# Convolution groups moved from the matrix engine to GpSimd and VectorE in a windowed attention with a gated unit

## The chip, the cores and the metric

One Trainium2 chip, one of its cores. A core has a matrix engine (TensorE, PE in the profile), VectorE (DVE), ScalarE (ACT), GpSimd (POOL) and SyncE (SP), which here only issues transfers. The metric is the device time of one execution in microseconds; lower is better. Times before are the median of three runs.

## The reference

Attention over 8 sequences, 8 heads, 576 positions, 64 dimensions, then a gated unit over the 512 joined channels:

```python
scores = (q @ k.T) / sqrt(64)
rel = pos[:, None] - pos[None, :]
mask_plain = (rel >= 0) & (rel < 32)                       # heads 0 to 3
mask_dil = (rel >= 0) & (rel < 128) & (rel % 4 == 0)       # heads 4 to 7
attn = softmax(where(mask, scores, -1e9))
x = (attn @ v).transpose(0, 2, 1, 3).reshape(B, S, 512)
gate_pre = sum_k conv_w[k] * x shifted by (4 - k) positions   # 5 taps, causal, one weight a channel
out = (sigmoid(gate_pre) * (x @ w_val)) @ w_out
```

Inputs and outputs are float32.

## The kernel before

The kernel is a list of 733 small tasks. Functions (`plain`, `dilated`, `attend`, `gated`, `outputs`, `weights`) add tasks to a plan in a fixed numbering, each with the engines that may run it, the tasks it depends on and the buffers it uses. `ORDER` then says, task by task, in which order and on which engine the instructions are written, and `HOMES` gives each buffer its place in a ring (`COUNTS` has the sizes: three double PSUM banks `ps2`, two single ones `ps1`, three `wt`, three `gate`, two `vp`, and so on). Each engine runs its tasks in that order; waits between engines follow from the buffers. A digit behind a P is a number of idle matmuls written ahead of the task.

Work is staged by pairs of sequences (g = 0 to 3). For each sequence the four plain and the four dilated heads are done two heads at a time:

- loads of q, k and v on SyncE's queue (lines 270 to 302; a large load waits for the fifth large load before it, `DEPTH`), transposes of q and k on TensorE into PSUM (L401 plain, L464 dilated), copies from PSUM into `qT` and `kT` on ScalarE (L312) or VectorE (L314). Dilated v is cast whole by GpSimd (`U`, into `vn`); plain v of the first four sequences is shifted and cast (`HA` to `HD`, into `vw`) by GpSimd or ScalarE (L316, L312).
- `attend`: scores (L333), exp on ScalarE (L340), the mask product on VectorE (L347, both inputs in SBUF), the product with v (L356), and the normalisation on VectorE (L365 reciprocal, L366 product). Transposes (L428, L488) and copies (`F` tasks) bring the result to `xT`, channels by positions.
- `gated`: for each pair the 1152 positions are cut in three blocks of 384 (four of 288 for the last pair), and each block in two channel pairs cp of two 128-channel chunks n. That makes 26 groups. In a group, `C` computes the five-tap convolution of both chunks as 20 matmuls of 64 x 64 diagonal weights (L530), `G` takes the tanh on ScalarE out of PSUM (L540), `V` is the projection in 8 matmuls (L548), and `Y` multiplies on VectorE (L558). Since channel halves lie crossed in the second chunk, its convolution also swaps partitions 0-63 and 64-127.
- `outputs`: 36 row blocks of four matmuls (L577), eviction by ScalarE (L584) or VectorE (L586), store on SyncE's queue (L590).

Weights are loaded through the `wt` buffers and cast by GpSimd (`Wv`, `Wo`).

Of the kernel before, what the change touches and what calls it, by code (L numbers as in the profile page):

```python
# [7 lines left out]
FP32 = mybir.dt.float32  # L8
BF16 = mybir.dt.bfloat16
# [7 lines left out]
0G 15S 16S 1S 13S 33P6 14S 34A 48S 17S 47S 49S 2P 31P1 32A 3V 18G 38P2 57P 51G 21P 59V 22V 53G 58V 52G 39A 40V  # L17
19P 35P 20A 26P2 36A 23P 80S 27A 37V 24A 28V 25V 41P2 54P 56A 4S 55A 42V 29P 30V 70P 81S 6G 45P3 5G 43P 50A
60P 73P 7S 46V 71A 44A 74A 8G 112S 61A 96P 84P 63P 64A 149P 72V 97A 75V 76P 98P 85V 65V 62V 82S 66P 77V 86P
67V 150A 99A 100P 78P 87A 101A 83G 103P 88P 89A 79V 68P 69V 104A 113S 105V 119P 114S 120A 91P 92A 145P 151P  # L20
93V 102V 90V 121A 94P 169S 146A 152V 106P 95V 147P 122P 107V 108P 170S 110P 123V 124A 138P 109A 201S 139A 148V
135P 185P 136A 125P 128P 129A 126A 111V 165P 166A 140V 130V 137V 116G 127V 186V 234S 202S 157P 158A 187P 115G
118G 117G 141P 171S 175P 176A 188V 192P 193A 131P 142V 132V 173P 172G 174A 189P 190A 208P 209V 210A 143P 133P
177P 178A 180P 203S 134V 211P 235S 250P 144V 159P 181A 213A 212A 227P 228A 153P 154A 11S 238P 205G 251V 194V
179V 191V 160V 182V 239A 206A 195P 229V 196V 207A 167P 168V 204G 12G 183P 184V 155P 252P 224P 225A 214P 240P
215A 9S 253V 156V 199P 254P 241V 255A 226V 217P 218A 161P 230P 197P 162A 200A 324S 267S 236S 216V 219V 245P
256V 220P 198A 246A 231V 10G 625P 628P 221V 323S 266S 325S 237G 626A 257P 242P 243A 276P 629A 222P 326G 223A
258A 278A 277V 163P 341P 232P 303P 247V 244V 259V 233V 342V 304A 299P 300A 164V 339P 260P 248P 329P 305P 330A
340V 268S 261V 631P 630S 355S 384S 533S 627S 346P 356S 249V 343P 264P 306V 265V 273P 632A 347A 344A 348V 274V
275A 272A 345V 262P 301P 302V 279P 280A 292P 634P 635V 263A 349P 350V 327P 293A 328A 289P 281V 282P 283A 290A  # L30
# [33 lines left out]
 'gate': 3,  # L64
 'osb': 5,
 'xT': 3,
 'yT': 3,
 'vw': 2,
 'wt': 3}
DEPTH = 5  # L70
NAT = 4


def hi_bf16(ap: bass.AP) -> bass.AP:
    b = ap.bitcast(BF16)
    idx = tuple([slice(None)] * (len(b.shape) - 1) + [slice(1, None, 2)])
# [632 lines left out]
```

## Time and profile before

| | us |
|---|---|
| median of three runs (lowest to highest) | 174.27 (173.8 to 174.28) |
| profiled execution | 173.37 |
| its span, first to last instruction | 171.7 |
| TensorE, matmuls busy | 153.0 |
| VectorE busy | 121.7 |
| ScalarE busy | 108.4 |
| GpSimd busy | 44.2 |

The mean granted clock of TensorE is 0.998. Transfers move 43.63 MB at a mean of 254 GB/s. Reading the rows: a group has its line, engine, operation, output and input tile, their shapes and the count; then total busy time and mean ns of one; then the engine's idle time just before, with what ended it. A row of the table by stage has the stage, its length, and for each engine the busy time and the count of instructions.

### The profile page before, as it was taken

The numbers are of one execution on the slowest core, as the hardware profiler recorded it, in microseconds if no ns is written. First come the engines' busy times: TensorE is split into PE (matmuls) and PEld (weight loads), VectorE is DVE, ScalarE is ACT, GpSimd is POOL, SyncE is SP. The second block draws the span as 40 slices with busy tenths as digits, with TensorE's granted clock in tenths as the row PEclk, the third lists the DMA queues.
The fourth block names the chain that finished last, engine by engine and source line by source line (L and its number), as shares of the span: only waits on it lengthen the run. The fifth ranks groups of instructions, "written<-read, shape, count | busy, mean of one in ns | idle before, by whom it ended". The sixth has DMA issues, their size and how long they took to land.

```text
span 171.7 us, 5752 instructions
## 1 busy us (share of the span) xinstructions
PE 153.0 (89%) x2441; PEld 102.2 (60%) x2460; DVE 121.7 (71%) x243; ACT 108.4 (63%) x182; POOL 44.2 (26%) x82
## 2 busy tenths in 40 slices
PE   6697967888989979899999799989999999999990
PEld 1355654677557546567766567576656577666640
DVE  6549778989899579779788658899368776664220
ACT  2147976198868744798847693888946675242542
POOL 7023998560659427403000000210110000000000
PEclk9999999999999999999999999999999999999999
DMA  4999999999799999999994948969979060333445
GB/s 137 325 355 290 375 370 210 311 374 319 200 383 364 362 269 281 373 353 222 282 328 139 267 115 286 373 165 390 270 202 303 2 244 4 116 119 138 186 165 199
DMA packets 49123, 43.63 MB, mean 254 GB/s; under 512 B 22981, under 2 KB 39365, under 8 KB 49098
## 3 DMA queue, kind: packets, MB, share of 16 engines
q1 hardware_dynamic: 49098, 43.27, 82.2%
q8 instruction: 19, 0.31, 0.7%
q14 instruction: 6, 0.05, 0.1%
HBM read 33.83 MB, written 9.44 MB: 252 GB/s over the span
## 4 chain that ended last, share of the span: by engine, by line
PE 58%; DMA 12%; DVE 11%; ACT 6%; SPq 5%; issue 3%; POOL 3%; ACTq 0%; DVEq 0%; POOLq 0%
PE pu L577 17%; PE pd L548 14%; PE pd L530 9%; DMA qk<-in_k_dram 5%; PE pd L356 5%; DVE et L347 4%; DMA wt<-in_moe_w_out_dram 4%; SPq L281 4%; PE pd L333 4%; DMA qk<-in_q_dram 3%; PE pu L464 3%; POOL w_out L316 3%; PE pd L401 2%; PE pu L488 2%; ACT et L340 2%
## 5 line engine op out<-in xcount | busy, mean ns | idle before, releaser
L340 ACT ACTIVATE et<-pd 128x576 bf16<-128x576 f32 x64 | 39.3, 657 | 10.4 <-PE pd L333 9.3
L347 DVE TENSOR_TENSOR et<-et,mask 128x576 bf16<-128x576 bf16 x64 | 33.9, 557 | 4.7 <-ACT et L340 4.5
L548 PE MATMUL pd<-xT,w_val 128*128 128x384 bf16 (+1 forms) x208 | 34.9, 313 | 0.7 <-DVE xn L366 0.4
L577 PE MATMUL pu<-w_out,yT 128*128 128x512 bf16 x127 | 33.4, 379 | 1.4 <-issue 0.6
L558 DVE SCALAR_TENSOR_TENSOR yT<-gate,pd 128x768 bf16<-128x768 bf16 (+1 forms) x26 | 23.0, 886 | 12.5 <-PE pd L548 8.5
L366 DVE TENSOR_TENSOR xn<-pd,rec 96x768 bf16<-96x768 f32 x32 | 30.5, 954 | 1.1
L316 POOL CAST vn<-vd 128x1536 bf16<-128x1536 f32 x8 | 12.3, 1540 | 70.3 <-DMA vd<-in_v_dram 70.3
L540 ACT ACTIVATE gate<-pd 128x768 bf16<-128x768 f32 (+1 forms) x26 | 19.9, 769 | 10.9 <-DVE yT L558 5.5
L548 PEld LDWEIGHTS <-w_val 128*128 128x128 bf16 x208 | 19.4, 97 | 11.6 <-issue 1.5
L530 PE MATMUL pd<-xT,conv_diag 64*64 64x384 bf16 (+1 forms) x520 | 23.1, 313 | 1.8 <-DVE xT L314 1.1
L584 ACT ACTIVATE osb<-pu 128x512 f32<-128x512 f32 x27 | 16.2, 601 | 11.0 <-PE pu L577 10.7
L577 PEld LDWEIGHTS <-yT 128*128 128x128 bf16 x144 | 12.6, 97 | 13.3 <-issue 1.1
L333 PE MATMUL pd<-qT,kT 64*128 64x96 bf16 x384 | 16.1, 209 | 3.1 <-ACT qT L312 0.9
L530 PEld LDWEIGHTS <-conv_diag 64*64 64x64 bf16 x520 | 15.1, 106 | 6.2 <-issue 2.5
L316 POOL CAST vw<-vp 32x384 bf16<-32x384 f32 (+2 forms) x31 | 16.8, 541 | 7.5 <-DMA vp<-in_v_dram 6.1
L356 PEld LDWEIGHTS <-et 128*128 128x128 bf16 x384 | 14.7, 97 | 6.5 <-DVE et L347 2.5
L464 PE MATMUL pu<-ident,qk 128*128 128x128 bf16 x160 | 14.8, 230 | 3.0 <-DMA qk<-in_k_dram 2.0
L333 PEld LDWEIGHTS <-kT 64*128 64x128 bf16 x384 | 10.1, 96 | 11.5 <-issue 6.3
L464 PEld LDWEIGHTS <-qk 128*128 128x128 bf16 x160 | 10.8, 102 | 7.3 <-DMA qk<-in_k_dram 3.0
L314 DVE COPY xT<-pu 128x576 bf16<-128x576 bf16 x18 | 10.1, 568 | 4.0 <-PE pu L488 3.1
L312 ACT COPY xT<-pu 128x576 bf16<-128x576 bf16 x14 | 8.9, 646 | 6.2 <-PE pu L428 3.6
L365 DVE RECIPROCAL rec<-pd 96x12 f32<-96x12 f32 x32 | 7.1, 223 | 7.6 <-PE pd L356 4.5
(52 smaller groups left out, 146.2 us busy)
## 6 DMA issues: line engine op xcount, KB each, us to landing
out_dram<-osb SPq DMA_DIRECT2D x36, 256.0 KB, 2.7
vd<-in_v_dram SPq DMA_DIRECT2D x8, 768.0 KB, 9.3
qk<-in_k_dram SPq DMA_DIRECT2D x8, 576.0 KB, 7.8
qk<-in_q_dram SPq DMA_DIRECT2D x8, 576.0 KB, 8.0
qk<-in_q_dram SPq DMA_DIRECT2D x6, 640.0 KB, 9.1
qk<-in_k_dram SPq DMA_DIRECT2D x6, 640.0 KB, 8.7
vp<-in_v_dram SPq DMA_DIRECT2D x4, 768.0 KB, 7.9
vp<-in_v_dram SPq DMA_DIRECT2D x4, 576.0 KB, 9.8
```

The source lines that it names most:

```text
L316: nc.gpsimd.tensor_copy(out_, in_)
L333: nc.tensor.matmul(out=ps2[ps.idx][:, l, QB * jj:QB * jj + QB], lhsT=kT[kt.idx][rb, c:c + 128], rhs=qT[qt.idx][rb, c:c + QB], start=True, ...
L340: nc.scalar.activation(out=et[e.idx][:, 0:2 * HW].rearrange("p (l n) -> p l n", l=2), in_=ps2[ps.idx][:, :, 0:HW], func=AF.Exp, scale=scale)
L347: (nc.vector if eng == DVE else nc.gpsimd).tensor_tensor(out=ev, in0=ev, in1=m, op=ALU.mult)
L356: nc.tensor.matmul(out=ps2[po.idx][:, hf, (2 * jj + l) * DA:(2 * jj + l + 1) * DA], lhsT=et[es[hf].idx][:, c:c + 128], rhs=val(j, l), star ...
L366: nc.vector.tensor_tensor(out=xn[xt.idx][0:QB].rearrange("p (h j) l d -> p h (j l) d", h=2), in0=a[:, :, :, 0:D], in1=rr[:, :, :, None].to ...
L464: nc.tensor.transpose(out=o[:, f:f + 128], in_=a[:, c * RD + 128 * cb:c * RD + 128 * cb + 128], identity=ident)
L530: nc.tensor.matmul(out=dst(ps2[pc.idx][64 * ob:64 * ob + 64, n, 0:wd]), lhsT=conv_diag[rb, 2 * cp + n, kk, :], rhs=mov(2 * cp + n, rb, c0 ...
L540: nc.scalar.activation(out=gate[gt.idx][:, :, 0:wd], in_=ps2[pc.idx][:, :, 0:wd], func=AF.Tanh, scale=0.5)
L548: nc.tensor.matmul(out=dst(ps2[pv.idx][:, n, 0:wd]), lhsT=w_val[:, mc, c * 128:(c + 1) * 128], rhs=mov(mc, slice(0, 128), c0), start=(mc = ...
L558: nc.vector.scalar_tensor_tensor(out=yT[yb.idx][:, 2 * cp:2 * cp + 2, t0:t0 + wd], in0=gate[gt.idx][:, :, 0:wd], scalar=1.0, in1=ps2[pv.id ...
L577: nc.tensor.matmul(out=ps1[po.idx], lhsT=yT[yb.idx][:, c, c0:c0 + 128], rhs=w_out[:, c, :], start=(c == 0), stop=(c == NCH - 1))
```

## The change

Eleven of the 26 groups, listed in `PCONV` as [pair, block, channel pair], no longer use TensorE for the convolution. Three tasks replace `C`: `Ka` sums the five taps of the first chunk, `Kb` the first four of the second, each on GpSimd or VectorE as the order says, into two `wt` buffers in float32; `Kc` adds the second chunk's last tap on VectorE and crosses its partition halves. On VectorE a tap is one scalar_tensor_tensor after a first tensor_scalar; on GpSimd it is a tensor_scalar and a tensor_tensor. `G` then reads the sums from SBUF. `V` of these groups no longer waits for the convolution. The convolution weights are kept in float32. The last number of each entry of SHIFTS is read by nothing in the kernel.

The eight loads of plain v are issued on ScalarE's queue instead of SyncE's, and no longer take part in the `DEPTH` rule. `ORDER` (now 755 tasks) and `HOMES` are new throughout. In the new order the 22 sums Ka and Kb are placed 13 on GpSimd (nine Ka, four Kb) and 9 on VectorE (two Ka, seven Kb); VectorE has four output evictions (nine before) and 25 of the copies out of PSUM (41 before), and ScalarE the rest.

```diff
-ORDER = (733 tasks)
+ORDER = (755 tasks)
...
 DEPTH = 5
+PCONV = [[0, 2, 1], [1, 0, 0], [1, 1, 0], [1, 1, 1], [1, 2, 0], [2, 0, 0], [2, 1, 0], [2, 1, 1], [2, 2, 0],
+ [3, 0, 0], [3, 1, 0]]
 NAT = 4
 
 
...
             assert eng in t.eng and not t.done and all(d.done for d in t.deps)
             for x in t.tens:
                 assert held.setdefault((x.cls, x.idx), x) is x
-            if t.load:
+            if t.load and eng == SP:
                 t.after = big[-DEPTH] if len(big) >= DEPTH else None
                 if t.big:
                     big.append(t)
...
     ident2 = consts.tile([128, D], BF16, name="ident2")
     ident_f = consts.tile([8, 8], FP32, name="ident_f")
     mask = [consts.tile([128, HW], BF16, name=f"mask{i}") for i in range(3)]
-    conv_w = consts.tile([128, NCH, K], BF16, name="conv_w")
+    conv_w = consts.tile([128, NCH, K], FP32, name="conv_w")
     conv_diag = consts.tile([128, NCH, K, D], BF16, name="conv_diag")
     w_val = consts.tile([128, NCH, Dm], BF16, name="w_val")
     w_out = consts.tile([128, NCH, Dm], BF16, name="w_out")
...
         nc.vector.memset(mask[1][0:80, QB + 48:2 * QB], 0.0)
 
 
-    def load(name, ten, issue, deps=(), big=True):
-        return plan.add(name, (SP,), lambda e: issue(), deps=deps, tens=[ten], load=True, big=big)
+    def load(name, ten, issue, deps=(), big=True, eng=SP):
+        return plan.add(name, (eng,), lambda e: issue(), deps=deps, tens=[ten], load=True, big=big)
 
     def load_p(src, b, ten, what):
         def issue():
...
                 o, a = vp[ten.idx][:, 0:18, 0:D], [[D, 128], [128 * D, 18], [1, D]]
             else:
                 o, a = vp[ten.idx][:, :, 0:D], [[D, 128], [QB * D, 4 * NB], [1, D]]
-            return nc.sync.dma_start(out=o, in_=src_ap(v, (b * H * S - (0 if nat else W)) * D, a))
-        return [load(f"Lvp{b}", ten, issue)]
-
-    SHIFTS = (("HA", ((1, 0, 64, 64, 0), (1, 64, 64, 0, 1)), 1.0),
-              ("HB", ((0, 0, 32, 96, -1), (0, 32, 32, 0, 0), (0, 64, 32, 32, 0)), 1.45),
-              ("HC", ((0, 96, 32, 64, 0), (2, 0, 32, 32, 1), (2, 32, 32, 64, 1)), 1.45),
-              ("HD", ((2, 64, 32, 96, 1), (2, 96, 32, 0, 2)), 1.0))
+            return nc.scalar.dma_start(out=o, in_=src_ap(v, (b * H * S - (0 if nat else W)) * D, a))
+        return [load(f"Lvp{b}", ten, issue, eng=ACT)]
+
+    SHIFTS = (("HA", ((1, 0, 64, 64, 0), (1, 64, 64, 0, 1)), 1.1),
+              ("HB", ((0, 0, 32, 96, -1), (0, 32, 32, 0, 0), (0, 64, 32, 32, 0)), 1.65),
+              ("HC", ((0, 96, 32, 64, 0), (2, 0, 32, 32, 1), (2, 32, 32, 64, 1)), 1.65),
+              ("HD", ((2, 64, 32, 96, 1), (2, 96, 32, 0, 2)), 1.1))
 
     def copy(eng, out_, in_):
         if eng == ACT:
...
                 return o.rearrange("p (h t) -> p h t", h=2) if both else o
 
             for cp in range(2):
-                pc, gt, pv = Ten("ps2"), Ten("gate"), Ten("ps2")
+                slow = [g, k, cp] in PCONV
+                pc, gt, pv = Ten("wt" if slow else "ps2"), Ten("gate"), Ten("ps2")
 
                 def conv(eng, cp=cp, pc=pc, c0=c0, mov=mov, dst=dst, wd=wd):
                     for kk in range(K):
...
                                     lhsT=conv_diag[rb, 2 * cp + n, kk, :],
                                     rhs=mov(2 * cp + n, rb, c0 + kk - (K - 1)),
                                     start=(kk == 0), stop=(kk == K - 1))
-                t_c = plan.add(f"C{g}{k}{cp}", (PE,), conv,
-                               deps=[x_done[(b, 2 * cp + n)] for b in last for n in range(2)] + [w_ready["conv"]],
-                               tens=[pc, gt, xb], out=pc)
-
-                def th(eng, pc=pc, gt=gt, wd=wd):
-                    nc.scalar.activation(out=gate[gt.idx][:, :, 0:wd], in_=ps2[pc.idx][:, :, 0:wd],
+                ka = Ten("wt")
+
+                def taps(eng, n, c=2 * cp, pc=pc, ka=ka, c0=c0, mov=mov, dst=dst, wd=wd):
+                    acc = dst((wt[ka.idx] if n else wt[pc.idx])[:, 0:wd])
+                    tmp = dst(wt[ka.idx][:, GW:GW + wd])
+                    for kk in range(K - n):
+                        x = mov(c + n, slice(0, 128), c0 + kk - (K - 1))
+                        w = conv_w[:, c + n, kk:kk + 1]
+                        if kk and eng == DVE:
+                            nc.vector.scalar_tensor_tensor(out=acc, in0=x, scalar=w, in1=acc, op0=ALU.mult, op1=ALU.add)
+                            continue
+                        e = nc.vector if eng == DVE else nc.gpsimd
+                        e.tensor_scalar(out=tmp if kk else acc, in0=x, scalar1=w, scalar2=None, op0=ALU.mult)
+                        if kk:
+                            e.tensor_tensor(out=acc, in0=acc, in1=tmp, op=ALU.add)
+
+                def last_tap(eng, c=2 * cp + 1, pc=pc, ka=ka, c0=c0, mov=mov, dst=dst, wd=wd):
+                    for lo, to in ((0, 64), (64, 0)):
+                        nc.vector.scalar_tensor_tensor(
+                            out=dst(wt[pc.idx][to:to + 64, GW:GW + wd]), in0=mov(c, slice(lo, lo + 64), c0),
+                            scalar=conv_w[lo:lo + 64, c, K - 1:K], in1=dst(wt[ka.idx][lo:lo + 64, 0:wd]),
+                            op0=ALU.mult, op1=ALU.add)
+                c_deps = [x_done[(b, 2 * cp + n)] for b in last for n in range(2)] + [w_ready["conv"]]
+                if slow:
+                    t_c = [plan.add(f"K{'ab'[n]}{g}{k}{cp}", (POOL, DVE), lambda e, n=n, taps=taps: taps(e, n),
+                                    deps=c_deps, tens=[pc, gt, xb, ka]) for n in range(2)]
+                    t_c.append(plan.add(f"Kc{g}{k}{cp}", (DVE,), last_tap, deps=t_c[1:], tens=[pc, gt, xb, ka]))
+                else:
+                    t_c = [plan.add(f"C{g}{k}{cp}", (PE,), conv,
+                               deps=c_deps, tens=[pc, gt, xb], out=pc)]
+
+                def th(eng, pc=pc, gt=gt, wd=wd, slow=slow):
+                    a = wt[pc.idx][:, 0:2 * GW].rearrange("p (n t) -> p n t", n=2) if slow else ps2[pc.idx]
+                    nc.scalar.activation(out=gate[gt.idx][:, :, 0:wd], in_=a[:, :, 0:wd],
                                          func=AF.Tanh, scale=0.5)
-                t_g = plan.add(f"G{g}{k}{cp}", (ACT,), th, deps=[t_c], tens=[pc, gt])
+                t_g = plan.add(f"G{g}{k}{cp}", (ACT,), th, deps=t_c, tens=[pc, gt])
 
                 def val(eng, cp=cp, pv=pv, c0=c0, mov=mov, dst=dst, wd=wd):
                     for n in range(2):
...
                                 rhs=mov(mc, slice(0, 128), c0),
                                 start=(mc == 0), stop=(mc == NCH - 1))
                 t_v = plan.add(f"V{g}{k}{cp}", (PE,), val,
-                               deps=[x_done[(b, c)] for b in last for c in range(NCH)] + w_ready["val"] + [t_c],
+                               deps=[x_done[(b, c)] for b in last for c in range(NCH)] + w_ready["val"] + (t_c if not slow else []),
                                tens=[pv, xb], out=pv)
 
                 def stt(eng, cp=cp, pv=pv, gt=gt, t0=t0, wd=wd):
```

69 lines of the change are left out of this document (35 added, 34 removed).

## The prediction

> **What bounds the kernel now.** I read the page's busy shares and its chain first, then busy time by stage, then the groups of instructions by shape.
>
> ```profile
> PE 153.0 (89%) x2441; PEld 102.2 (60%) x2460; DVE 121.7 (71%) x243; ACT 108.4 (63%) x182; POOL 44.2 (26%) x82
> PE 58%; DMA 12%; DVE 11%; ACT 6%; SPq 5%; issue 3%; POOL 3%; ACTq 0%; DVEq 0%; POOLq 0%
> core 0: us, PE busy (x) PEld busy (x) DVE busy (x) ACT busy (x) POOL busy (x), PEclk, DMA share, GB/s
> 0.00:12.55 12.55, 9.33 (x64) 4.91 (x65) 7.00 (x42) 3.73 (x5) 3.82 (x13) 1.00 0.82 272
> 12.55:40.00 27.45, 22.55 (x457) 16.30 (x458) 23.25 (x42) 19.50 (x34) 18.98 (x44) 1.00 1.06 323
> 40.00:100.00 60.00, 54.53 (x953) 37.68 (x960) 47.14 (x85) 43.52 (x75) 18.23 (x24) 1.00 0.99 291
> 100.00:164.45 64.45, 63.21 (x960) 41.94 (x967) 44.34 (x77) 38.65 (x66) 3.15 (x2) 1.00 0.63 195
> 164.45:171.70 7.25, 3.35 (x16) 1.38 (x15) 0.01 (x1) 2.99 (x5) 0.00 (x0) 0.95 0.47 181
> ```
>
> TensorE holds 58% of the chain. From 100 to 164.45 us it is busy 63.21 of 64.45 us (98%), so there it is the limit; from 12.55 to 40 us it is busy 82%, and the DMA share is at its ceiling. VectorE, the second engine, has room: 114.73 us busy (23.25 + 47.14 + 44.34) in the 151.9 us between its first mask and its last product. GpSimd is nearly unused after 70 us. All this is in an execution of 171.7 us span that took 173.37 us, 1.7 us beside the span; the median of the runs is 174.27, 0.9 above it. So a span from my sums becomes a forecast by adding 2.6.
>
> **TensorE: what is taken off.**
>
> ```profile
> L530 PE MATMUL pd<-xT,conv_diag 64*64 64x384 bf16 x360 | 17.6, 326 | 1.8 <-DVE xT L314 1.1 <-DVE kT L314 0.3 <-ACT et L340 0.2
> L530 PE MATMUL pd<-xT,conv_diag 64*64 64x288 bf16 x160 | 5.5, 284 | 0.0
> ```
>
> A convolution group is 20 matmuls. The 18 groups of 384 columns cost 17.6/18 = 0.98 us each, the 8 of 288 cost 0.69. The list takes nine wide and two narrow groups: 9 x 0.98 + 2 x 0.69 = 10.2 us, so TensorE falls from 153.0 to 142.8. With its 18.7 us of idle time unchanged the span would be 161.5: that is the most this edit can give, unless the new order removes idle time as well. Each group also stops holding one of the three double PSUM buffers. I give that nothing, since the late stage was already 98% full.
>
> **VectorE: what is put on.** Decoding the new order by task: of the 11 groups, the first chunk's five taps (Ka) run on GpSimd in nine and on VectorE in two (one wide, one narrow); the second chunk's first four taps (Kb) on GpSimd in four and on VectorE in seven (six wide, one narrow); the crossed last tap (Kc, two instructions) always on VectorE. In exchange VectorE gives away five output evictions (9 to 4) and 16 PSUM copies: 3 into kT and 2 into qT from the plain heads, 3 into qT from the dilated heads, 8 into xT.
>
> ```profile
> L558 DVE SCALAR_TENSOR_TENSOR yT<-gate,pd 128x768 bf16<-128x768 bf16 x18 | 17.1, 948 | 6.5 <-PE pd L548 6.4
> L558 DVE SCALAR_TENSOR_TENSOR yT<-gate,pd 128x576 bf16<-128x576 bf16 x8 | 5.9, 748 | 5.9 <-ACT gate L540 3.8 <-PE pd L548 2.1
> L586 DVE TENSOR_SCALAR osb<-pu 128x512 f32<-128x512 f32 x9 | 6.2, 685 | 2.2 <-PE pu L577 2.2
> L314 DVE COPY xT<-pu 128x576 bf16<-128x576 bf16 x18 | 10.1, 568 | 4.0 <-PE pu L488 3.1 <-PE pu L428 0.5 <-ACT et L340 0.3
> L314 DVE COPY kT<-pd 128x576 bf16<-128x576 bf16 x6 | 4.5, 754 | 5.6 <-PE pu L428 3.1 <-PE pd L401 2.2 <-ACT kT L312 0.3
> L314 DVE COPY qT<-pd 128x576 bf16<-128x576 bf16 x3 | 2.3, 750 | 0.0
> L314 DVE COPY qT<-pu 128x576 bf16<-128x576 bf16 x8 | 3.6, 450 | 1.7 <-PE pu L464 1.4 <-ACT osb L584 0.3
> 112.28 0.44 DVE L314 COPY qT<-pu 128x576 bf16<-128x576 bf16 x1
> 112.64 0.44 DVE L347 TENSOR_TENSOR et<-et,mask 128x576 bf16<-128x576 bf16 x1
> ```
>
> A tap on VectorE is a scalar_tensor_tensor. Its two sizes in the trace give (948 - 748)/192 = 1.04 ns per element, so 548 ns for 384 and 448 for 288. The first tap of a sum is a tensor_scalar with an SBUF source: between about 300 ns (the 450 ns copy of 576, scaled) and 550 (the 685 ns eviction, scaled); I take 450, and 400 when narrow. Then Kb is 450 + 3 x 548 = 2.09 us (narrow 1.74), Ka 2.64 (2.19), Kc 1.10 (0.90). Sum: 6 x 2.09 + 1.74 + 2.64 + 2.19 + 9 x 1.10 + 2 x 0.90 = 30.8 us in 60 instructions. The last two rows start 0.36 us apart though each lasts 0.44: neighbours overlap by 0.07, so 30.8 - 60 x 0.07 = 26.6 us. Taken away: 5 x 0.685 + 3 x 0.754 + 2 x 0.750 + 3 x 0.450 + 8 x 0.568 = 13.1 us, less 21 x 0.07, = 11.6. VectorE goes to 121.7 + 26.6 - 11.6 = 136.7 us.
>
> **What GpSimd's new work does to VectorE.** This term decides.
>
> ```profile
> L347 DVE TENSOR_TENSOR et<-et,mask x64: 441/452/1720, 12.6 to 145.2; 128x576 bf16<-128x576 bf16 x64
> 110.27 2.08 DVE L347 TENSOR_TENSOR et<-et,mask 128x576 bf16<-128x576 bf16 x2
> 110.37 1.68 POOL L316 CAST vn<-vd 128x1536 bf16<-128x1536 f32 x1 [29.55 <-DMA vd<-in_v_dram]
> 12.00:70.60 58.60, 17.30 (x29) 1.00 1.05 317
> 70.60:150.00 79.40, 16.61 (x35) 1.00 0.78 230
> 27.50:37.50 10.00, 4.07 (x6) 1.00 0.96 289
> 70.60:110.00 39.40, 8.24 (x18) 1.00 0.90 266
> 12.00:70.60 58.60, 36.30 (x67) 1.00 1.05 317
> 70.60:150.00 79.40, 4.61 (x3) 1.00 0.78 230
> ```
>
> The mask product, the one VectorE operation here with two SBUF inputs, takes 452 ns at the median and up to 1720. Two of them needed 2.08 us just when GpSimd ran a 1.68 us cast. The other rows group this: busy time of the mask line on VectorE in four windows, then GpSimd's in two. With GpSimd 62% busy (36.30 of 58.60) a mask costs 17.30/29 = 0.597 us; with GpSimd quiet, 8.24/18 = 0.458. So a two-input operation loses 0.14 us on average beside GpSimd's casts, and 0.22 in the densest stretch (4.07/6 = 0.678).
>
> The Trainium skill says this more harshly (SBUF — State Buffer, section "Who interferes with whom"): a VectorE instruction with two SBUF inputs and a GpSimd instruction that reads SBUF exclude each other, and the later one waits out the other entirely. The 2.08 us pair agrees; the 0.14 average says that short casts leave gaps.
>
> After the change GpSimd works until the last groups. The 35 late masks go from 16.61/35 = 0.475 to about 0.597: + 4.3 us. The two-input taps on VectorE (7 x 3 + 2 x 4 + 22 = 51) pay 0.14 each: + 7.1. VectorE then stands at 148.1; with no blocking at all 136.7, at the 0.22 rate 155.6.
>
> **GpSimd's own load.**
>
> ```profile
> L316 POOL CAST vn<-vd 128x1536 bf16<-128x1536 f32 x8 | 12.3, 1540 | 70.3 <-DMA vd<-in_v_dram 70.3
> L316 POOL CAST w_out<-wt 128x512 bf16<-128x512 f32 x1 | 0.6, 614 | 1.7 <-DMA wt<-in_moe_w_out_dram 1.7
> L316 POOL CAST w_val<-wt 128x128 bf16<-128x128 f32 x8 | 2.2, 316 | 0.1
> ```
>
> One-input work of 384 elements lies between the last two: about 0.50 us. A two-input add is nowhere in the trace: at least 0.50, and 1.0 if its operands are read one after the other. I take 1.0. Nine Ka (one narrow) and four Kb (one narrow) are then 8 x 6.5 + 5.1 + 3 x 5.0 + 3.8 = 76 us, and GpSimd goes to about 120, 98 with the low price: no bound either way. By the Trainium skill (GPSIMD Engine Reference, section 3.1) a two-input operation needs about 2.6 cycles per element, an estimate of 0.83 us here; no run so far shows it, and it changes nothing above.
>
> **ScalarE and the queues.**
>
> ```profile
> L584 ACT ACTIVATE osb<-pu 128x512 f32<-128x512 f32 x27 | 16.2, 601 | 11.0 <-PE pu L577 10.7
> L312 ACT COPY xT<-pu 128x576 bf16<-128x576 bf16 x14 | 8.9, 646 | 6.2 <-PE pu L428 3.6 <-PE pu L488 2.6
> L302 SPq DMA_DIRECT2D vp<-in_v_dram x8: 367/439/1007, 5.0 to 126.1; - x8
> 38.26 5.67 SPq L281 DMA_DIRECT2D qk<-in_k_dram  x1
> ```
>
> ScalarE takes over 5 x 0.60 + 16 x 0.65 = 13.4 us of evictions and eight issues of plain v at 0.44 us: 108.4 becomes about 125. It gains slack nowhere but is not the bound. The shifted casts only change places (nine on ScalarE before, eight after). On SyncE the eight loads leave the five-deep chain of large loads, so up to one more load is in flight. Up to 100 us the DMA share is 0.82 to 1.06 already, so I give this nothing; the worst case is a rival below.
>
> **The sum.** VectorE needs 148.1 us. Of these 7.0 lie in the first 12.55 us; then 141.1 remain, with 12.55 us before and 7.25 after them in which VectorE cannot work on heads or products. An in-order engine that is the bound still waits: TensorE idled 2% in its dense stage and 9% from 40 to 100 us; I take 5%. Span: 141.1/0.95 + 19.8 = 168.3; with the 2.6, **170.8 us**. TensorE's 142.8 us fits under that with 25 us idle. What is late next is thus VectorE.
>
> **Rivals.**
> *TensorE stays the bound.* If the taps slip between GpSimd's instructions, VectorE needs 136.7 and the span is TensorE's 161.5: 164.1 us. For it: the 18 masks from 70.6 to 110 us at 0.458. Against: GpSimd was idle then. Chance 0.14.
> *The shared path to SBUF eats the gain: slower.* One mechanism: each two-input VectorE instruction waits for GpSimd's current tap. At 0.22 us for 35 masks and 51 taps VectorE needs 155.6: 148.6/0.95 + 19.8 + 2.6 = 178.8 us. It decides from 151.3 us of VectorE work on, that is 0.17 us per operation, only 0.03 above what I take. For it: the 2.08 us pair; and GpSimd's adds may last 1.0 us, twice the casts that gave 0.14. By the Trainium skill's lock (the section above) it would be this case; the short casts so far speak half against. Chance 0.22.
> *VectorE stands behind GpSimd.* In four groups Kb is on GpSimd, and Kc sits in VectorE's queue waiting for it; behind Kc stand masks and normalisations, for which TensorE's attention products wait. The next group's taps also wait until a tanh has freed one of three wt buffers. If GpSimd is late by 1.5 us (three one-input taps) at each of the four places, VectorE is held for 6 us more: (148.1 + 6 - 7)/0.95 + 19.8 + 2.6 = 177.2. For it: GpSimd's adds have no price in the trace. Against: 40 us of slack on GpSimd. Chance 0.10.
> *ScalarE stands behind an issue.* A large load held SyncE's queue 5.67 us when too much was in flight. If two of the eight issues do that on ScalarE, exponentials are late by 2 x 5.2 = 10.4 us; with half of it hidden, 176. Against: ScalarE has one such load at a time. Chance 0.06.
>
> **The numbers.** A difference under 0.3% can't be told from none here. The forecast has 0.48: 0.38 of it faster by more than that, 0.07 within, 0.03 slower. Faster: 0.38 + 0.14 = 0.52; same 0.07; slower 0.03 + 0.22 + 0.10 + 0.06 = 0.41. The range goes from the TensorE bound, 164, to just beyond the costlier rivals, 180. The likeliest case alone goes from 166.4 (VectorE waits 2%) to 177.5 (9%).
>
> **What would show it.** Right: 300 matmuls left on the convolution line and TensorE near 143 us; VectorE over 145 us and the largest share of waits for its results; late masks near 0.6 us; GpSimd between 98 and 120. Wrong: masks near 0.46 throughout (first rival), masks or taps 0.2 us or more over their size (second), VectorE idle before Kc because of GpSimd (third), ScalarE issues of several us (fourth). If TensorE is again 98% busy in the last 60 us, my bound was wrong.

## The result, and the profile after

The changed kernel takes 237.11 us (median of four runs, 235.68 to 237.62) against 174.06 for the kernel before: a ratio of 1.361, 95% interval 1.354 to 1.368. The forecast was 170.8 us, with a range from 164 to 180. The profiled execution of the changed kernel took 235.68 us, with a span of 234.0. Some executions run at a lower granted clock and take longer; where a kernel had both kinds, its time below is that of the faster ones, and the traces of b2 and d2 are of slower ones.

First the page of the kernel after: busy time of each engine, then the chain that ended last, by engine.

```profile
PE 162.6 (69%) x2241; PEld 104.8 (45%) x2241; DVE 159.6 (68%) x282; ACT 120.2 (51%) x202; POOL 174.5 (75%) x192
POOL 43%; DVE 19%; PE 14%; DMA 11%; issue 7%; ACT 4%; SPq 1%; POOLq 0%; ACTq 0%; DVEq 0%
```

GpSimd, which held 3% of the chain before, now holds 43%. TensorE went from 58% to 14%, although it is busy longer than before with 200 fewer matmuls recorded. The table by stage, from the same view as before, says why.

```profile
44.00:75.00 31.00, 24.75 (x386) 17.17 (x389) 24.47 (x37) 21.97 (x39) 27.30 (x34) 0.85 0.59 193
93.00:195.00 102.00, 67.27 (x868) 40.97 (x867) 70.10 (x104) 52.33 (x89) 95.65 (x78) 0.85 0.50 147
195.00:216.00 21.00, 18.20 (x239) 12.19 (x239) 18.16 (x30) 10.85 (x18) 16.23 (x17) 0.80 0.17 64
```

From 93 to 195 us GpSimd is busy 95.65 of 102 us (94%), while TensorE (67.27) and VectorE (70.10) both have a third of the stage idle. The last columns are the granted clock, the DMA share and GB/s: the clock is 0.80 to 0.85 in these stages, where it was 1.00 before, and the remaining matmuls last longer (367 ns on the mean for a projection matmul of 384 columns, 325 before). The groups of GpSimd's instructions, and those of VectorE's taps and masks (L551 is the multiplication of a tap on GpSimd, L553 its addition):

```profile
L551 POOL TENSOR_SCALAR wt<-xT,conv_w 128x384 f32<-128x384 bf16 (+1 forms) x61 | 80.2, 1320 | 8.8 <-ACT xT L315 3.9 <-DVE wt L557 1.2
L553 POOL TENSOR_TENSOR wt<-wt,wt 128x384 f32<-128x384 f32 (+1 forms) x36 | 36.8, 1023 | 3.0
L553 POOL TENSOR_TENSOR wt<-wt 128x384 f32<-128x384 f32 (+1 forms) x12 | 12.3, 1024 | 1.0
L548 DVE SCALAR_TENSOR_TENSOR wt<-xT,conv_w,wt 128x384 f32<-128x384 bf16 x22 | 20.2, 920 | 0.8
L350 DVE TENSOR_TENSOR et<-et,mask 128x576 bf16<-128x576 bf16 x64 | 36.8, 602 | 8.4 <-ACT et L343 8.1
```

The 61 multiplications were counted right (13 sums, 48 later taps) but last 1.32 us each instead of 0.50; the 48 additions last the 1.0 us that was taken. GpSimd's taps are 80.2 + 36.8 + 12.3 = 129.3 us where the forecast had 76. Two views of the waits: who waited for whom (total, times, longest), and from the chain in order of time the piece with plain v.

```profile
ACT gate L572 <- POOL wt L553: 21.2, 4, 9.8
PE pd L359 <- POOL vn L319: 20.2, 5, 7.0
POOL vw L319 <- DMA vp<-in_v_dram: 12.7, 1, 12.7
DVE wt L557 <- POOL wt L553: 9.6, 3, 6.5
```

```profile
27.26 16.29 DMA vp<-in_v_dram
```

Tanh waits for sums (21.2 us), and TensorE's attention product waits 20.2 us for casts of dilated v: those casts stand behind taps in GpSimd's queue. One load of plain v takes 16.29 us from its issue, on the chain.

### The profile page after: what moved, and what is told of

It reads as the page before. It is cut to its first block, busy times and chain, and to the rows that moved or that the text cites. A ratio compares the mean times of both kernels' runs of the same rounds, so it can differ in the third digit from the quotient of the medians.

```text
span 234.0 us, 5514 instructions
## 1 busy us (share of the span) xinstructions
PE 162.6 (69%) x2241; PEld 104.8 (45%) x2241; DVE 159.6 (68%) x282; ACT 120.2 (51%) x202; POOL 174.5 (75%) x192
## 4 chain that ended last, share of the span: by engine, by line
POOL 43%; DVE 19%; PE 14%; DMA 11%; issue 7%; ACT 4%; SPq 1%; POOLq 0%; ACTq 0%; DVEq 0%
POOL wt L551 25%; POOL wt L553 15%; DMA vp<-in_v_dram 7%; DVE et L350 5%; PE pu L609 4%; DVE wt L548 4%; PE pd L580 4%; DMA qk<-in_k_dram 4%; DVE wt L557 3%; DVE yT L590 2%; DVE xn L369 2%; POOL vn L319 2%; POOL vw L319 2%; PE pu L467 2%; ACT et L343 2%
## 5 line engine op out<-in xcount | busy, mean ns | idle before, releaser
L551 POOL TENSOR_SCALAR wt<-xT,conv_w 128x384 f32<-128x384 bf16 (+1 forms) x61 | 80.2, 1320 | 8.8 <-ACT xT L315 3.9
L580 PE MATMUL pd<-xT,w_val 128*128 128x384 bf16 (+1 forms) x208 | 40.2, 342 | 11.2 <-ACT xT L315 6.1
L350 DVE TENSOR_TENSOR et<-et,mask 128x576 bf16<-128x576 bf16 x64 | 36.8, 602 | 8.4 <-ACT et L343 8.1
L609 PE MATMUL pu<-w_out,yT 128*128 128x512 bf16 x144 | 39.5, 405 | 0.0
L553 POOL TENSOR_TENSOR wt<-wt,wt 128x384 f32<-128x384 f32 (+1 forms) x36 | 36.8, 1023 | 3.0
L580 PEld LDWEIGHTS <-w_val 128*128 128x128 bf16 x208 | 20.9, 104 | 25.1 <-issue 16.3
L557 DVE SCALAR_TENSOR_TENSOR wt<-xT,conv_w,wt 64x384 f32<-64x384 bf16 (+1 forms) x22 | 19.1, 866 | 10.1 <-POOL wt L553 9.6
L359 PE MATMUL pd<-vn,et 128*128 128x65 bf16 x192 | 10.6, 212 | 21.9 <-POOL vn L319 20.2
L548 DVE SCALAR_TENSOR_TENSOR wt<-xT,conv_w,wt 128x384 f32<-128x384 bf16 (+1 forms) x29 | 24.8, 857 | 1.0
L336 PE MATMUL pd<-qT,kT 64*128 64x96 bf16 x384 | 17.7, 212 | 4.8 <-DVE yT L590 1.7
L572 ACT ACTIVATE gate<-wt 128x768 bf16<-128x768 f32 (+1 forms) x11 | 9.0, 819 | 23.3 <-POOL wt L553 21.2
L319 POOL CAST vn<-vd 128x1536 bf16<-128x1536 f32 x8 | 12.3, 1535 | 11.1 <-DMA vd<-in_v_dram 11.1
L404 PE MATMUL pd<-ident,qk 128*64 128x128 bf16 x288 | 12.6, 249 | 8.8 <-ACT et L343 8.7
L315 ACT COPY xT<-pu 128x576 bf16<-128x576 bf16 x22 | 14.0, 641 | 7.0 <-PE pu L431 5.2
```

The costliest lines, as they stand in the source:

```text
L319: nc.gpsimd.tensor_copy(out_, in_)
L350: (nc.vector if eng == DVE else nc.gpsimd).tensor_tensor(out=ev, in0=ev, in1=m, op=ALU.mult)
L359: nc.tensor.matmul(out=ps2[po.idx][:, hf, (2 * jj + l) * DA:(2 * jj + l + 1) * DA], lhsT=et[es[hf].idx][:, c:c + 128], rhs=val(j, l), star ...
L548: nc.vector.scalar_tensor_tensor(out=acc, in0=x, scalar=w, in1=acc, op0=ALU.mult, op1=ALU.add)
L551: e.tensor_scalar(out=tmp if kk else acc, in0=x, scalar1=w, scalar2=None, op0=ALU.mult)
L553: e.tensor_tensor(out=acc, in0=acc, in1=tmp, op=ALU.add)
```

## The experiments

My first theory after the result: the multiplication on GpSimd was priced from the wrong rows, and plain v's new queue costs the rest. The rival: GpSimd's instructions are as short as predicted, but VectorE's two-input work and GpSimd hold each other up.

**The prices by themselves (p1_price).** The kernel before, with 45 GpSimd instructions added at the end of GpSimd's queue, where VectorE has few masks left.

```diff
     plan.run()
+    for _ in range(5):
+        nc.gpsimd.tensor_scalar(out=xf, in0=xb_, scalar1=s1, scalar2=None, op0=ALU.mult)
...
+    for _ in range(5):
+        nc.gpsimd.tensor_tensor(out=xf2, in0=xf, in1=yf, op=ALU.add)
```

> The kernel before, with 45 extra GpSimd instructions at the end of its queue (they start near 126 us, beside few masks), five each of nine forms, 384 elements unless said: multiply by a per-partition scalar bf16 to f32, the same by a constant, per-partition f32 to f32, copy bf16 to f32, copy f32 to bf16, add of two f32, per-partition bf16 to bf16, per-partition with 192 elements, multiply bf16 by f32 tensors. Theory price (the tap instruction itself is slow on GpSimd): the per-partition multiply takes about 1.24 us here too, against about 0.5 for the copies; the add 1.0. Rival lock (the 1.24 to 1.37 us of the changed kernel are waits for VectorE's hold on SBUF): 0.5 to 0.6 us here. If the price is per element, 192 elements take about 0.65.

Its groups of GpSimd's instructions, by shape:

```profile
L685 POOL TENSOR_SCALAR wt<-warm,zsc 128x384 f32<-128x384 bf16 x5 | 6.2, 1245 | 0.5
L687 POOL TENSOR_SCALAR wt<-warm 128x384 f32<-128x384 bf16 x5 | 6.0, 1190 | 0.4
L695 POOL TENSOR_TENSOR wt<-wt,wt 128x384 f32<-128x384 f32 x5 | 5.0, 997 | 0.3
L699 POOL TENSOR_SCALAR wt<-warm,zsc 128x192 f32<-128x192 bf16 x5 | 3.8, 765 | 0.4
L691 POOL CAST wt<-warm 128x384 f32<-128x384 bf16 x5 | 2.6, 518 | 0.3
```

A copy of 384 elements lasts 518 ns, just as the casts said. The multiplication, also with one tensor as input, lasts 1245 ns, and its five executions differ by 4 ns. The rest of the kernel still runs beside them, but the eight masks on VectorE from 126 to 146 us, beside multiplications, take 3.24 us together, no more each than with GpSimd quiet. From 192 to 384 elements the multiplication grows by 480 ns; by these two sizes it is 2.5 ns per element and about 285 fixed. The price theory holds; no wait for VectorE is needed to explain the 1245 ns.

**GpSimd's sums cut to their first tap (a1_onetap, a4_onetap_vpsync).** The output lacks the other taps of the 13 sums. The second also issues plain v on SyncE's queue again.

```diff
-                    for kk in range(K - n):
+                    for kk in range(1 if eng == POOL else K - n):
```

> The changed kernel, but a sum that GpSimd computes takes only its first tap (part of the convolution is left out). GpSimd loses 48 multiplies at 1.32 us and 48 adds at 1.02, 112 us of 174. Theory price: GpSimd's length was the bound, so the time falls from 237 to 180 to 195 us. Rival stalls (late plain v, SyncE held by a wt buffer, an order that does not fit): the time stays above 205 us, and TensorE and VectorE idle where they idled before.

> Both at once: GpSimd's sums take one tap only (part of the convolution is left out) and plain v is on SyncE's queue. If price and plain v are the two causes and they add, 185.7 less 12 (237 to 225 with plain v alone): 172 to 177 us, at the kernel before. If the 12 us only moved GpSimd's chain forward, nothing is left to gain with a short chain: 183 to 187.

184.14 us, as the price theory said, and 169.87 with plain v on SyncE, 2 us under what I expected, a ratio to before of 0.974 (0.963 to 0.985). So without 48 of GpSimd's taps, and with plain v's queue as it was, the rest of the change runs, and a little faster than before. GpSimd's later taps, with all that they do to the other engines, and plain v's queue hold the whole loss.

**Plain v back on SyncE's queue (a2_vpsync).**

```diff
-            return nc.scalar.dma_start(out=o, in_=src_ap(v, ...))
-        return [load(f"Lvp{b}", ten, issue, eng=ACT)]
+            return nc.sync.dma_start(out=o, in_=src_ap(v, ...))
+        return [load(f"Lvp{b}", ten, issue)]
```

> The changed kernel with plain v issued on SyncE's queue again, in the five-deep chain, at the same places of the order. If ScalarE's queue made the second load of plain v late (16.3 us from issue to landing, GpSimd waiting 12.7 and ScalarE 9.0 for it), it lands in about 9 us, and since GpSimd's taps come behind it 6 to 9 us come back: 228 to 231. If the DMA engines were simply full, nothing changes: 235 to 239.

224.97 us, ratio 1.293 (1.285 to 1.301): 12.1 us less than the changed kernel, more than I had expected. GpSimd is now more than half of the chain that ended last:

```profile
POOL 56%; PE 15%; DVE 14%; issue 6%; DMA 4%; ACT 2%; SPq 1%; POOLq 0%; ACTq 0%; DVEq 0%
```

**Own buffers for the weights (a3_wt5).** The weight loads get two `wt` buffers of their own, and the sums keep three.

```diff
- 'wt': 3}
+ 'wt': 5}
...
+            if x in self.own:
+                x.idx = 3 + self.own.index(x) % 2
```

> The changed kernel with five wt buffers, two of them for the weight loads alone. In the changed kernel SyncE issues nothing between 37.4 and 59.8 us: the last w_out load waits 14.9 us for a tap buffer, and later q, k and v loads stand behind it. Theory price: GpSimd has its own chain of 174 us and the early stall costs 0 to 4 us: 233 to 237. Rival stalls: 10 us or more come back: under 227.

236.97 us, ratio 1.362 (1.341 to 1.384): no difference from the changed kernel, as the price theory said.

**GpSimd at the predicted prices (c1_copytap, c2_copytap_vpsync).** The multiplication on GpSimd becomes a copy (0.5 us, as forecast); the weights are left out of these sums. The second has plain v on SyncE's queue. If price were all, both would come near the versions with one tap.

```diff
-                        e.tensor_scalar(out=tmp if kk else acc, in0=x, ...)
+                        if eng == POOL:
+                            e.tensor_copy(tmp if kk else acc, x)
+                        else:
+                            e.tensor_scalar(out=acc, in0=x, ...)
```

> The changed kernel with each GpSimd multiply replaced by a copy of the same tile (the weights of those taps are left out). The copy took 0.52 us and the add 1.00 at the end of the earlier run, the very prices of the prediction, so GpSimd should be busy near 126 us. Theory price: the GpSimd price is the step that failed, and what is left is the prediction's sum of 170.8 plus the cost of plain v on ScalarE's queue: 180 to 190 us. Rival lock: masks and taps on VectorE meet GpSimd as often as before, VectorE needs over 155 us, and the time stays above 195.

> Taps on GpSimd at the prices of the prediction (copy 0.52, add 1.00; their weights left out) and plain v on SyncE's queue: the prediction's world without plain v. If price and plain v were the only errors, the prediction's sum holds: 168 to 175 us. Theory lock: in the run with copies VectorE was busy 166.8 us, not 148, the masks at a median of 0.67 us and the taps 0.74; that stays when plain v moves, so the time is 208.4 less 12, 193 to 199 us.

208.37 us (207.51 to 209.23) and 197.62 (ratio 1.137, 1.130 to 1.145). The first lies over the 180 to 190 us of the price theory, the second is what the lock theory gave. Price is not all: 28 us stand between 197.62 and the 169.87 of the version with one tap. VectorE's busy time has them. First, of c2, the busy times, the chain that ended last and one stage; then TensorE's waits for masks, three of VectorE's groups (the mask, a tap, the crossed tap), and the shortest, median and longest crossed tap in ns. Then the busy times and the same three groups in a4:

```profile
PE 155.8 (79%) x2241; PEld 99.1 (50%) x2241; DVE 166.5 (85%) x282; ACT 120.1 (61%) x202; POOL 135.7 (69%) x192
DVE 56%; PE 22%; issue 9%; DMA 8%; ACT 3%; SPq 1%; ACTq 0%; DVEq 0%
100.00:150.00 50.00, 37.16 (x494) 21.92 (x492) 47.99 (x61) 31.75 (x54) 46.09 (x53) 0.93 0.69 197
PEld L359 <- DVE et L350: 11.9, 11, 2.6
PE pd L359 <- DVE et L350: 9.1, 9, 2.5
L350 DVE TENSOR_TENSOR et<-et,mask 128x576 bf16<-128x576 bf16 x64 | 42.0, 683 | 0.4 <-ACT et L343 0.2
L548 DVE SCALAR_TENSOR_TENSOR wt<-xT,conv_w,wt 128x384 f32<-128x384 bf16 x22 | 20.8, 944 | 0.8
L560 DVE SCALAR_TENSOR_TENSOR wt<-xT,conv_w,wt 64x384 f32<-64x384 bf16 x18 | 17.6, 980 | 0.4
L560 DVE SCALAR_TENSOR_TENSOR wt<-xT,conv_w,wt x22: 511/761/1781, 46.9 to 178.8; 64x384 f32<-64x384 bf16 x18, 64x288 f32<-64x288 bf16 x4
```

```profile
PE 147.6 (88%) x2241; PEld 96.4 (58%) x2241; DVE 139.9 (84%) x282; ACT 119.1 (71%) x202; POOL 65.0 (39%) x96
L350 DVE TENSOR_TENSOR et<-et,mask 128x576 bf16<-128x576 bf16 x64 | 30.6, 506 | 0.7 <-ACT et L343 0.6
L548 DVE SCALAR_TENSOR_TENSOR wt<-xT,conv_w,wt 128x384 f32<-128x384 bf16 x22 | 15.0, 683 | 0.8
L557 DVE SCALAR_TENSOR_TENSOR wt<-xT,conv_w,wt 64x384 f32<-64x384 bf16 x18 | 11.5, 637 | 0.4
```

VectorE runs the same 282 instructions in both, 26.6 us longer beside GpSimd's copies and additions. These three groups alone explain 42.0 - 30.6 + 20.8 - 15.0 + 17.6 - 11.5 = 23.3 of it. From 100 to 150 us both engines are full (47.99 and 46.09 of 50), but the chain tells them apart: VectorE holds 56% of it and GpSimd nothing, and for the attention product TensorE's weight loads wait 11.9 us and its matmuls 9.1 for masks, against 2.8 for GpSimd's casts. So in this version VectorE is the bound, as forecast for the change, and it pays the toll of the second rival. The longest crossed tap, 1781 ns where the mean in a4 is 637, began 0.08 us after a cast of dilated v of 1.46 us.

**All 22 sums on VectorE (e1_alldve).** Nothing is added on GpSimd; plain v stays on ScalarE's queue.

```diff
-Ka and Kb on GpSimd in ORDER (13 words ending in G)
+the same words ending in V
```

> The changed kernel with all 22 sums on VectorE, at the same places of the order. VectorE gets 13 more sums, nine of about 2.6 us and four of about 2.1, 32 us, and loses its waits for GpSimd (taps 0.82 at the median against 0.52 at least). Theory price: GpSimd's slow taps were the bound, so even a VectorE of 170 to 180 us is better: 195 to 210 us. Rival (the groups are too much work for any engine but TensorE, wherever they go): 225 us or more.

226.41 us, ratio 1.298 (1.286 to 1.311): I had given 195 to 210. VectorE is busy 176.1 us, and with GpSimd quiet its taps of 384 elements last 626 ns on the mean (group below), not the 944 of c2. That is nearly a tap's own price, 0.08 us above the 548 ns that I took.

```profile
L548 DVE SCALAR_TENSOR_TENSOR wt<-xT,conv_w,wt 128x384 f32<-128x384 bf16 x63 | 39.4, 626 | 2.2
```

**Only the queue of plain v or of dilated v changed (b1_vpact, b2_vdact).** The kernel before, with nothing else of the change. The loads also leave the chain of five. In b2 it is dilated v, whose rows are 1024 bytes where plain v has 256.

```diff
-            return nc.sync.dma_start(out=o, in_=src_ap(v, ...))
+            return nc.scalar.dma_start(out=o, in_=src_ap(v, ...))
```

> The kernel before with plain v alone moved to ScalarE's queue, at the same places of its order and outside the five-deep chain. If ScalarE's queue as such is the cost (issue behind exponentials, more large loads in flight), plain v lands later than 9.1 us at the median and the time rises by 3 to 12 us. If the cost came from where the new order put the issues, it stays within 1 us of 174.

> The kernel before with dilated v, not plain v, on ScalarE's queue, at the same places of its order and outside the chain of five. Dilated v comes in rows of 1024 bytes, plain v in rows of 256 (21632 packets for 5.51 MB). Theory turns: two queues take turns by packet, so the queue with small packets gets a small share; plain v took up to 17.7 us to land from ScalarE's queue, dilated v should land in 6 to 10 us, and the time stays within 8 us of 174. Rival (any load on ScalarE's queue is issued late and lands late): 14 to 18 us to landing at the worst places, and 190 us or more.

b1 takes 205.43 us (204.45 to 206.33), ratio 1.179 (1.169 to 1.189): 31 us for eight loads that only change their queue, where I had given 3 to 12. From its chain in order of time, then its largest waits, then its list of transfers (KB each, median us from issue to landing), and last the landing of plain v, before and in b1:

```profile
5.89 17.73 DMA vp<-in_v_dram
31.99 16.30 DMA vp<-in_v_dram
```

```profile
POOL vw L316 <- DMA vp<-in_v_dram: 52.4, 4, 19.0
vp<-in_v_dram ACTq DMA_DIRECT2D x4, 768.0 KB, 5.9
vp<-in_v_dram ACTq DMA_DIRECT2D x4, 576.0 KB, 14.2
DMA to landing us min/median/max: 5.8/9.1/11.2
DMA to landing us min/median/max: 5.5/7.5/17.7
```

An issue on ScalarE lasted 0.37 to 0.43 us, so it does not block the engine. The first two loads, among SyncE's large ones, took 17.7 and 16.3 us to land; the second was issued at 31.99 us, where SyncE had issued it at 22.43. In ScalarE's in-order queue it stands behind shift casts that wait for the load before. GpSimd then waits 52.4 us for plain v. b2 takes 182.11 us: dilated v lands in 4.9 to 9.9 us there, no slower than before (8.2 to 10.7), and the time still rises by 8 us, the most that I allowed. Its loads are issued later than before, the second at 21.60 us instead of 17.73, the sixth at 89.17 instead of 68.91, and TensorE waits 11.4 us for its casts. So a queue change can cost without slow landing, most likely by the late issue; for the rows of 256 bytes slow landing is added. What leaving the chain of five does by itself was not run. The Trainium skill (DMA: Bandwidth & Descriptors, section "Queues, rings and completion order") says that each transfer engine takes turns between queues packet by packet; a queue of small packets beside one of large packets would then move few bytes. The landing times of b1 and b2 agree, but no run here separates the packet size from everything else.

**A few groups in the order of before (d1_five, d2_three).** Five and three groups, first chunk on GpSimd, the rest on VectorE, plain v on SyncE's queue, a fourth `wt` buffer.

```diff
+PCONV = [[1, 2, 0], [2, 0, 0], [2, 1, 0], [3, 0, 0], [3, 3, 0]]     # d1
+PCONV = [[1, 2, 0], [2, 0, 0], [3, 0, 0]]                           # d2
```

> The kernel before, its order and its loads kept, with five groups only taken off TensorE ([1,2,0], [2,0,0], [2,1,0], [3,0,0], [3,3,0]) where GpSimd is idle: Ka on GpSimd (about 11 us each), Kb and Kc on VectorE at the place where the convolution stood. TensorE loses 3 x 0.98 + 2 x 0.69 = 4.3 us, VectorE gains 16 us. If TensorE alone is the bound after 100 us and GpSimd is in time: 170 to 172 us. If tanh must wait for GpSimd, or masks and taps for the shared path: 174 to 178.

> The same with three groups, [1,2,0], [2,0,0] and [3,0,0]. TensorE loses 2.65 us: 171.5 to 173 if nothing waits; with GpSimd late for tanh at one of the places, 174 to 175.

199.69 us (ratio 1.149, 1.144 to 1.153) and 186.46 (1.069, 1.062 to 1.076), both misses. In the trace of d2 a cast of dilated v began at 95.55 us instead of 79.36: it stood behind a sum before which GpSimd had waited 13.6 us for VectorE. I took this queue for the cause, and tested that next.

**Casts ahead of the sums; no sum on GpSimd (d3_casts_first, d4_two_dve).** Two groups, [1, 2, 0] and [2, 0, 0], with tanh and products placed later. In d3 each sum stands behind the cast; in d4 the same sums run on VectorE.

> The kernel before with two wide groups moved off TensorE ([1,2,0] and [2,0,0]), plain v on SyncE's queue; GpSimd sums only their first chunk, each of the two sums placed BEHIND the casts of dilated v in GpSimd's queue, and tanh and products of the two groups placed later. Theory (three and five groups cost 13 and 27 us because the casts of dilated v stood behind sums in GpSimd's in-order queue): casts at about 79 and 110 us as before, 171.5 to 176 us. Rival (any GpSimd sum beside VectorE's two-input operations is what costs): over 179 us, with masks between 80 and 125 us at 0.6 us or more.

> The same two groups in the same places, with the first chunk's sums on VectorE too, so nothing is added on GpSimd. TensorE gives up 2.0 us, VectorE takes on 2 x 5.8 us of taps in a stretch (80 to 125 us) where it is about 70% busy. Theory: 172 to 176 us, within 2 us of the version with GpSimd. Rival (GpSimd's sums are what costs): 172 to 176 us while the version with GpSimd is over 179.

181.57 us (1.045, 1.042 to 1.048) and 186.15 (1.071, 1.068 to 1.075). Both theories fall: the casts of d3 were in time at 80.70 and 111.73 us, and it is over 179 us all the same, as its rival said (its 17 masks from 80 to 125 us took 0.61 us on the mean, 0.50 before). But the rival falls too: the version without any GpSimd sum is the slower one, by 4.6 us. TensorE's and VectorE's timelines of d4 show where it goes (start, length; in brackets TensorE's idle time and what ended it), then one stage of its table by stage:

```profile
115.18 2.58 DVE L558 SCALAR_TENSOR_TENSOR wt<-xT,conv_w,wt 128x384 f32<-128x384 bf16 x4
117.67 0.45 DVE L358 TENSOR_TENSOR et<-et,mask 128x576 bf16<-128x576 bf16 x1
118.04 0.45 DVE L325 COPY qT<-pu 128x576 bf16<-128x576 bf16 x1
118.55 0.69 PE L475 MATMUL pu<-ident,qk 128*128 128x128 bf16 x5 [2.87 <-DVE qT L325]
100.00:125.00 25.00, 17.20 (x268) 11.76 (x260) 19.16 (x38) 13.64 (x24) 1.47 (x1) 0.86 0.84 259
```

The same stage of the kernel before:

```profile
100.00:125.00 25.00, 24.18 (x425) 16.24 (x426) 18.99 (x35) 19.91 (x35) 2.88 (x2) 1.00 0.90 268
```

Four taps run 2.58 us without a break, the copy into `qT` stands behind them in VectorE's queue, and TensorE stands 2.87 us until it comes. In this stage TensorE is busy 17.20 us where it was 24.18, while VectorE is no fuller than before. Of TensorE's idle time in the stage, 7.2 us in five waits end with a result of VectorE, the 2.87 us among them; not all of these results stood behind taps, and the granted clock is lower too (0.86). TensorE has no slack later to win it back: it was 98% busy from 100 us on. The same order with tanh and products placed later and the convolutions still on TensorE was not run, so what the moved tasks cost by themselves is not shown.

**The new order with none, three, six and nine groups (f1 to f4).** The changed kernel's order and evictions, plain v on SyncE's queue, and the other groups back on TensorE, as matmuls placed where their tanh stood, with buffers taken where one is free.

```diff
+PCONV = []                                                             # f1
+PCONV = [[1, 2, 0], [2, 1, 1], [3, 0, 0]]                              # f2
+PCONV = [[0, 2, 1], [1, 1, 0], [1, 2, 0], [2, 1, 1], [2, 2, 0], [3, 0, 0]]   # f3
+PCONV = (the eleven without [1, 1, 1] and [2, 0, 0])                   # f4
```

> The changed kernel's order with none of its groups on GpSimd and VectorE: all 26 convolution groups are matmuls again, each placed where its tanh stood, and plain v goes through SyncE's queue. What is left of the change is the order and the share of evictions. Theory (the sums and plain v's queue are what costs, the order by itself little): 172 to 180 us with TensorE at 153 us. Rival (the order itself is worse): over 190 us.

> As the one before, with three wide or narrow groups ([1,2,0], [2,1,1], [3,0,0]) left on GpSimd and VectorE at the places that the changed order has for them: three sums on GpSimd, three on VectorE, six crossed taps. TensorE 150 us. Theory now (a block of taps in VectorE's in-order queue is paid nearly in full, since masks and normalisations behind it hold TensorE): 4 to 10 us over the version with no group. Rival (in an order made for it the sums hide): within 2 us of it, or faster.

> The changed kernel's order, plain v on SyncE's queue, with six groups ([0,2,1], [1,1,0], [1,2,0], [2,1,1], [2,2,0], [3,0,0]) on GpSimd and VectorE: one sum of each on GpSimd, the other and the crossed tap on VectorE. GpSimd about 110 us. If sums hide as long as GpSimd has slack, each group goes on giving about its 1 us: 174 to 176.5 us. Rival (what slows VectorE grows with GpSimd's load from the start): over 181 us.

> As the one before with nine groups (all but [1,1,1] and [2,0,0], the two whose sums are both on GpSimd). GpSimd about 140 us, in a stretch from 50 to 165 us. Theory (beyond some GpSimd load the sums come late, and VectorE and TensorE stand behind them): 185 to 205 us, so the two groups with both sums on GpSimd would be 20 to 40 of the 51 us that the changed kernel loses with plain v on SyncE. Rival (each group costs about the same): about 212 us.

| groups moved | us | ratio to before (95%) |
|---|---|---|
| 0 (f1) | 181.24 | 1.041 (1.036 to 1.047) |
| 3 (f2) | 178.04 | 1.024 (1.019 to 1.029) |
| 6 (f3) | 189.75 | 1.089 (1.080 to 1.099) |
| 9 (f4) | 207.59 | 1.195 (1.188 to 1.203) |
| 11 (a2) | 224.97 | 1.293 (1.285 to 1.301) |

Busy time of the engines in f1, f2 and f4:

```profile
PE 153.7 (86%) x2439; PEld 101.5 (57%) x2461; DVE 107.3 (60%) x222; ACT 119.3 (67%) x202; POOL 45.5 (25%) x83
PE 151.3 (86%) x2380; PEld 100.3 (57%) x2401; DVE 118.7 (67%) x241; ACT 119.4 (68%) x202; POOL 72.9 (41%) x108
PE 158.2 (77%) x2260; PEld 103.0 (50%) x2281; DVE 155.8 (76%) x278; ACT 120.0 (58%) x202; POOL 137.6 (67%) x160
```

At its own places in its own order a small share of the change does gain: three groups take TensorE from 153.7 to 151.3 us and the time from 181.2 to 178.0, which I had forecast as a loss of 4 to 10. Part of this gain may come from where I put the matmuls in f1; that was not tested. From the third group to the sixth each costs 3.9 us, from there to the ninth 5.9, and the last two, which have both sums on GpSimd, 8.7 each. For six groups the rival came true. For nine the time lies between my 185 to 205 and the rival's 212: the loss grows with each group from the third on, and does not come all at once at some load. The order alone, with the matmuls where I put them, is 4% slower than the order of before, just over the 172 to 180 that I gave; a better place for them was not looked for. No complete version in these runs beats the kernel before.

## Why the prediction was wrong

From the runs with plain v on SyncE the loss can be walked in steps: 174.1 before; 169.9 with GpSimd's later taps left out; 197.6 with them at the predicted price; 225.0 at their true price; 237.1 with plain v on ScalarE's queue. (The terms of the forecast's own sum add up to 170.9, not 170.8.)

**TensorE's relief: right in kind.** Three groups (two wide, one narrow) gave 2.4 us of the 2.65 that the forecast's prices give. Over all, TensorE went to 147.6 us in a4, not 142.8, and to 162.6 in the changed kernel, where its granted clock was lower. It did not matter, since it was no longer the bound.

**GpSimd's own load: the step that failed first, +27 us (225.0 against 197.6).** "One-input work of 384 elements lies between the last two: about 0.50 us" took casts for all work with one tensor as input. A copy is 518 ns, a multiplication by a weight 1245. That turned 76 us into 129, and "no bound either way" into an engine that is 94% busy for 102 us, with tanh, casts and attention products behind it. The addition, where I saw no row and said so, was right (997 ns in p1; 1.0 taken). The estimate from the Trainium skill (GPSIMD Engine Reference, section 3.1) was 0.83 us, which the measurement exceeds by a fifth. The bound from both sides was drawn round the unknown addition and not round the multiplication, which had no row either: the trace of before has no multiplication on GpSimd.

**What GpSimd does to VectorE: right mechanism, size too small, +28 us (197.6 against 169.9).** This step alone would have put the time out of the range, at 197.6 us with GpSimd at the price of the forecast. The forecast gave 11.4 us: 0.14 for 35 masks and 51 taps. At the predicted prices VectorE paid 26.6 us more than in a4, and a4 already had some: 0.18 on each of the 64 masks, 0.26 to 0.34 on each tap of 384 elements. First taps on VectorE, with one tensor as input, for which the forecast had no toll, went from 413 to 695 ns. With the measured 139.9 us (a4) and 166.5 us (c2) in place of VectorE's 148.1, the forecast's sum gives 162.3 and 190.3: some 7 us too little for both, but their distance is the 28 us that was measured. The 0.14 came from a stage with GpSimd 62% busy; in c2 it was 92% busy where VectorE worked hardest (46.09 of 50 us). The densest row I had, 0.22, was put into a rival and should have been the middle. A tap's own price was low as well: 626 ns with GpSimd quiet, 548 taken. By the lock of the Trainium skill (SBUF — State Buffer, section "Who interferes with whom") each tap could wait for a whole GpSimd instruction. On the mean a tap in c2 lost 0.32 us against e1 (944 and 626), less than one GpSimd copy of 0.5; the longest crossed tap lost 1.1 us against the mean of a4, beside a cast of 1.46. So the lock's direction is borne out, and waits of nearly a whole instruction occur; as the price of every tap a whole instruction would be too much.

**Plain v's queue: "I give this nothing" cost 12.1 us (237.1 against 225.0).** I looked at the share of the transfer engines and at the 0.44 us of an issue. I did not ask what the issue stands behind on ScalarE, nor what else is in flight when it lands. The fourth rival had the right engine with a wrong mechanism: no issue lasted several us. In the order of before, the same edit costs 31 us.

**The rivals.** The second had the sign and the mechanism of the second step, at 178.8 us. The third (VectorE stands behind GpSimd) is seen: VectorE waits 9.6 us before crossed taps, and it was priced at 6; but tanh and TensorE wait more (21.2 and 20.2 us). The sum took one engine for the bound and added 5% for waits. d4 shows what that leaves out: with VectorE no fuller than before, TensorE was busy 7 us less in one stage, and for 2.87 us of that it stood behind a block of taps.

**What stays open.** Whether the 16 us landings of plain v come from packet size or from the order of the requests; what the queue and leaving the chain of five each cost; why TensorE in a4 keeps 4.8 us more than forecast; and whether three groups in an order made for just those would beat the kernel before.

## What to carry to other kernels

Price an instruction from rows of the same operation on the same engine; where the trace has only a copy, the operation has no price, and the range must be drawn round it. A toll measured beside a lightly used neighbour does not hold once the change fills that neighbour: work it out again at the load that the change itself makes. A transfer moved to another queue needs two looks, at what it stands behind there and at what is in flight beside it, even if the transfer engines have the same bytes to move.

## What was not expected of the hardware

- On GpSimd a multiplication of 384 bfloat16 elements by a weight (1245 ns) lasts longer than an addition of two tensors (997) and more than twice as long as a copy (518); a constant in place of the weight changes little (1190).
- TensorE's granted clock fell to 0.80 to 0.85 on the mean of three stages of the changed kernel, in which TensorE idled 13 to 34% of the time, and its busy time rose to 162.6 us with fewer matmuls. The mean hides stretches: it was 0.50 from 87.3 to 93.9 us and 1.00 from 94.1 to 124.6.
- Eight loads with rows of 256 bytes on a second queue, outside the chain of five, cost 31 us in the kernel before; the slowest took 17.7 us to land, where on the shared queue the slowest took 11.2.
